# The first expert routing of a fused attention and two-layer expert kernel, cut into more steps and spread over one more attention round, with two elementwise parts on GpSimd

## The chip, the cores and the metric

One core of a Trainium2 chip runs the whole program. The metric is the device time of one execution in microseconds (us). The core has a matrix engine (TensorE, PE in the rows; PEld is its weight load), VectorE (DVE), ScalarE (ACT), GpSimd (POOL) and SyncE (SP), each with its own in-order instruction queue, and 16 DMA engines that they feed. The kernel's gathers by index are issued from GpSimd's queue.

## What is computed

```python
def _attn_ref(q, k, v, w_phi):                 # 4 batches, 8 heads, 576 tokens, 64 wide
    def phi(x):
        proj = np.einsum('bhsd,df->bhsf', x, w_phi)                  # 128 features
        proj = proj - np.max(np.abs(proj), axis=-1, keepdims=True)
        return np.concatenate([np.exp(proj), np.exp(-proj)], axis=-1)
    q_p, k_p = phi(q), phi(k)
    kv = np.einsum('bhsf,bhsd->bhfd', k_p, v); z = np.sum(k_p, axis=2)
    num = np.einsum('bhsf,bhfd->bhsd', q_p, kv)
    return num / (np.einsum('bhsf,bhf->bhs', q_p, z)[..., None] + 1e-06)

def _moe_ref(x, modality_id, w_gate, modality_bias, w1, w2):   # 2304 tokens, 512 wide, 8 experts
    logits = x @ w_gate + modality_bias[modality_id]
    e_idx = np.argmax(logits, axis=1)                          # one expert per token
    gate_w = softmax(logits)[e_idx]
    for e in range(8):
        h = np.maximum(x[e_idx == e] @ w1[e], 0.0)             # 1024 hidden
        out[e_idx == e] = gate_w * (h @ w2[e])

def _moe2_ref(x, w_a, w_b, w_out):                             # 1536 hidden
    return ((x @ w_a) * (x @ w_b)) @ w_out
```

## The kernel before

The program has three phases. **Attention** runs in rounds `r` = 0 to 8 (`Attn.round`). Each handles one unit `u` (a batch pair and a pair of heads): round `r` does the first half of unit `r` (`phi`, `turn`, `kx`, and `num` parts (0,0) and (0,1)) and the second half of unit `r - 1` (`num` parts (1,0), (1,1), (2,0), then `store`). Units 0 to 3 are the tokens of half 0, units 4 to 7 those of half 1. In this phase TensorE's instructions go out in the order in which the code writes them; the other engines' orders are set by a scheduler from the dependences and priorities.

In `phi`, TensorE writes `pjp`, VectorE takes its largest magnitude (`m`, L156) and subtracts it (`df`, L157), and ScalarE takes exponentials; `turn` transposes `df` on TensorE (`qtp`, L187) and ScalarE makes `qts`; `kx` multiplies (`kxp`, L211) and VectorE copies the result out (`kx`, L214); `vg` computes the gate's share (`vgp`, copied to `v`, L199); `num` multiplies (`nmp`, L231) and VectorE divides (`rec`, `x`, L237 to L242); `store` sends `x` to DRAM as `xs` and adds the gate's logits on GpSimd (`lgp`, L259 and L261). `kxp`, `vgp`, `nmp` and the routing's `rkp` share two PSUM buffers.

The **routing** of half 0 (class `Route`) is worked in between these rounds. Its steps are `start`, `gate` (bias by modality), `score` (largest logit, one-hot `oh`), `rank` (a running count by matmul, `rkp`), `place` (tile starts), `where` (each token's row `pl` and column `col`), `bounds` (the numbers `meta` that tell each tile's expert and rows, and the sorted place `cq`, `cl`), `table` (a matmul of one-hots, `tbp`, that yields `idx`, the token that stands in each row) and `back` (the same for the way back, `tbq`, that yields `perm` and the gate weights). `onehot` builds the one-hots of `table` and `back` for half 0 on GpSimd, nine instructions each: `tbpl`, `tbph` for the table, `tbql`, `tbqh` for the way back; `tbpr` and `tbqr` are their products with the token numbers. A side table says after which part of which round a step is written: `aside(0)` follows `kx` of the old unit, `aside(1)` follows its `num` and `store`, `aside(2)` ends the round. `late` keeps a step's instructions behind the last `kx` copy (`at.copied`), with a lower priority.

In the **first expert layer** (`Moe`), a tile of 608 rows is fetched by five gathers `xg` (L577, GpSimd's queue, rows of `xs` by `idx`), transposed on TensorE (`mxt`, L589), split on ScalarE and VectorE (`mxh`, `mxl`) and multiplied (`hp`, `yp`) with weights `s` that SyncE loads by `meta`. Half 1 is routed during this phase, on VectorE. In the **second layer** (`Moe2`) TensorE runs `abp` and `op`. The transposes of the first tile are put into the attention's last part: the first stands behind `kxp` of round 7, ahead of that round's last `nmp`.

Of the kernel before, what the change touches and what calls it, by code (L numbers as in the profile page):

```python
# [58 lines left out]
class Attn:  # L59
# [159 lines left out]
    def num(self, u, *parts):  # L219
# [20 lines left out]
        for b, h in parts:  # L240
            k = 4 if b < 2 else 2
            nc.vector.tensor_mul(x[:, 4 * b:4 * b + 4, h, :] if b < 2 else x[:, 8, :, :], ps[:, o:o + k, 0:72],  # L242
                                 rec[:, o:o + k].unsqueeze(2).to_broadcast([P, k, 72]))
            o += k
# [91 lines left out]
class Route:  # L336
    def __init__(self, tc, pool, lgp, bs, bp):
        self.tc, self.nc = tc, tc.nc
        self.pool, self.lgp, self.bs, self.bp = pool, lgp, bs, bp
# [798 lines left out]
```

## Time and profile before

| | |
|---|---|
| median of 3 runs (lowest to highest) | 821.34 us (820.34 to 823.38) |
| the profiled execution's own time | 816.26 us |
| its span in the profile | 814.5 us |
| busy share of PE, DVE, ACT, POOL | 98%, 74%, 46%, 16% |
| attention until the first `hp` | 163.4 us |
| mean granted TensorE clock | 0.997 of full speed |

The span runs from the first to the last instruction that the profile shows; the execution's own time is 1.8 us longer. Times in the rows are microseconds from the span's start.

### The profile page before, as it was taken

What the parts mean: (1) busy time and instruction counts of PE and PEld (TensorE: products, weight loads), DVE (VectorE), ACT (ScalarE), POOL (GpSimd) and SP (SyncE); (2) the same over time, 40 slices, a digit from 0 to 9 for tenths busy, and PEclk for the clock granted to TensorE, in tenths of its full rate; (3) what the DMA queues carried; (4) which work ended last, traced back from release to release, by engine and by line L of the source; (5) the groups of instructions that cost most, each with busy time, mean ns of one, the idle gap of its engine ahead of it and who ended that gap; (6) DMA issues with size and microseconds to landing.
All of it is one profiled execution on the core that took longest, in us unless ns stands there. A gap on an engine that the chain in (4) does not pass through costs nothing.

```text
span 814.5 us, 18323 instructions
## 1 busy us (share of the span) xinstructions
PE 796.5 (98%) x7284; PEld 750.3 (92%) x7284; DVE 602.4 (74%) x1071; ACT 376.0 (46%) x666; POOL 134.1 (16%) x164
## 2 busy tenths in 40 slices
PE   8999998999999999999999999999999999999996
PEld 6999898899999999999999899999999999999995
DVE  6888899799999999972798787864455686544553
ACT  4556544545345646443554434643333364333333
POOL 2000009532245532200220100030000002000002
PEclk9999999999999999999999999999999999999998
DMA  8665442586589887761889787785566658665642
GB/s 296 211 187 172 153 123 72 150 276 230 200 280 354 325 283 277 265 240 66 329 302 353 257 301 268 259 285 197 189 222 211 201 182 299 210 202 191 211 133 88
DMA packets 85164, 184.22 MB, mean 226 GB/s; under 512 B 27761, under 2 KB 37521, under 8 KB 85073
## 3 DMA queue, kind: packets, MB, share of 16 engines
q1 hardware_dynamic: 81872, 173.21, 62.1%
q0 software_dynamic: 3040, 9.72, 3.4%
q8 instruction: 58, 0.95, 0.5%
q14 instruction: 34, 0.27, 0.1%
q10 hardware_dynamic: 160, 0.07, 0.0%
HBM read 145.21 MB, written 37.75 MB: 225 GB/s over the span
## 4 chain that ended last, share of the span: by engine, by line
PE 32%; issue 16%; DVE 1%; ACT 1%; DMA 1%; POOL 1%; POOLq 0%; DVEq 0%
PE abp L54 7%; PE abp L56 7%; PE abp L55 7%; PE op L55 4%; PE op L54 4%; PE op L56 4%; DMA raw<-in_moe_w 1%; POOL out L853 1%; ACT pc L897 0%; DVE gl L885 0%; ACT gh L884 0%; DVE ca L883 0%; ACT yh L797 0%; DVE o L850 0%; POOLq L1135 0%
## 5 line engine op out<-in xcount | busy, mean ns | idle before, releaser
L897 ACT COPY pc<-abp 128x384 f32<-128x384 f32 x252 | 120.6, 479 | 189.9 <-PE abp L56 187.3
L54 PE MATMUL abp<-yh,fw 128*128 128x384 f32 x504 | 170.0, 337 | 2.7 <-ACT pc L897 1.7
L56 PE MATMUL abp<-yh,fw 128*128 128x384 f32 x504 | 170.0, 337 | 0.0
L55 PE MATMUL abp<-yl,fw 128*128 128x384 f32 x504 | 169.8, 337 | 0.0
L54 PEld LDWEIGHTS abp<-yh,fw 128*128 128x128 f32 x504 | 94.6, 188 | 12.0 <-ACT pc L897 2.7
L55 PEld LDWEIGHTS abp<-yl,fw 128*128 128x128 f32 x504 | 94.7, 188 | 7.5
L56 PEld LDWEIGHTS abp<-yh,fw 128*128 128x128 f32 x504 | 94.6, 188 | 0.0
L717 POOL TENSOR_SCALAR cvs<-cvs 128x768 f32<-128x768 f32 x24 | 58.1, 2419 | 198.9 <-ACT cvs L716 198.9
L55 PE MATMUL op<-fw,gh 128*128 128x512 f32 x216 | 85.6, 397 | 0.0
L54 PE MATMUL op<-fw,gh 128*128 128x512 f32 x216 | 85.1, 394 | 0.0
L56 PE MATMUL op<-fw,gl 128*128 128x512 f32 x216 | 85.0, 393 | 0.0
L55 PE MATMUL yp<-hl,wh 128*128 128x304 f32 x256 | 77.4, 303 | 0.6 <-DVE hl L608 0.6
L54 PE MATMUL hp<-mxh,wh 128*128 128x304 f32 x256 | 77.9, 305 | 0.0
L55 PE MATMUL hp<-mxl,wh 128*128 128x304 f32 x256 | 77.8, 304 | 0.0
L56 PE MATMUL hp<-mxh,wl 128*128 128x304 f32 x256 | 77.7, 304 | 0.0
L56 PE MATMUL yp<-hh,wl 128*128 128x304 f32 x256 | 77.6, 304 | 0.0
L54 PE MATMUL yp<-hh,wh 128*128 128x304 f32 x256 | 77.0, 303 | 0.0
L853 POOL DMA_INDIRECT out<-o,perm x18 | 18.4, 1020 | 332.8 <-ACT o L852 326.0
L190 ACT ACTIVATE qts<-qtp 128x512 f32<-128x512 f32 (+1 forms) x80 | 38.3, 558 | 57.8 <-PE qtp L187 49.6
L908 DVE TENSOR_TENSOR d<-u,pc 128x768 f32<-128x768 f32 x36 | 34.5, 957 | 29.1 <-ACT pc L897 29.1
L885 DVE TENSOR_TENSOR gl<-ca,gh 128x384 fp32r<-128x384 f32 x72 | 39.9, 559 | 19.9 <-ACT gh L884 19.0
L884 ACT CAST gh<-ca 128x384 fp32r<-128x384 f32 x72 | 36.7, 514 | 36.5 <-DVE ca L883 36.4
(191 smaller groups left out, 1599.0 us busy)
## 6 DMA issues: line engine op xcount, KB each, us to landing
fw<-wsc SPq DMA_DIRECT2D x72, 512.0 KB, 4.3
fw<-wsc SPq DMA_DIRECT2D x144, 256.0 KB, 3.4
raw<-in_moe_w SPq DMA_DIRECT2D x24, 768.0 KB, 6.1
s<-in_moe_w SPq DMA_DIRECT2D x32, 512.0 KB, 5.0
fw<-wsc SPq DMA_DIRECT2D x72, 128.0 KB, 2.9
wsc<-whi SPq DMA_DIRECT2D x12, 640.0 KB, 6.3
wsc<-wsum SPq DMA_DIRECT2D x12, 640.0 KB, 7.0
wsc<-whi SPq DMA_DIRECT2D x12, 512.0 KB, 3.2
```

Of the source, the lines that this page charges most:

```text
L54: nc.tensor.matmul(out, lh, rh, start=start, stop=False)
L55: nc.tensor.matmul(out, lh, rl, start=False, stop=False)
L56: return nc.tensor.matmul(out, ll, rh, start=False, stop=stop).ins
L190: nc.scalar.activation(t[:, s, :n, :], ps[:, :n, :], AF.Exp, scale=1.0 - 2.0 * s)
L717: nc.gpsimd.tensor_scalar(out=s.bitcast(F32), in0=s.bitcast(F32), scalar1=LEAST, scalar2=None, op0=ALU.max)
L853: st = nc.gpsimd.indirect_dma_start(out=self.out[:, :], out_offset=bass.IndirectOffsetOnAxis(ap=self.routes[bp].perm[:, c:c + 1], axis=0), ...
L884: nc.scalar.copy(gh, ca[:, i, :])
L885: self.gl = nc.vector.tensor_sub(gl, ca[:, i, :], f32(gh)).ins
L897: copied = nc.scalar.copy(x, ps).ins
L908: nc.vector.tensor_add(d, u, x.unsqueeze(1).to_broadcast([P, 2, n]))
```

## The change

`Route.steps` has twelve steps instead of nine. `place` makes one of the two prefix sums; the other goes with the spans' comparisons and differences to the new step `spans`. The sorted place goes to `sort`, and `bounds` keeps the reductions that make `meta`. The gate's normaliser and its split into three bf16 parts go from `rank` and `back` to `norm`. For half 0, `eng` is GpSimd: seven of `gate`'s eight instructions and five of `spans` run there (`b2` is two instructions instead of one, and the product has a tile `span` of its own). Half 1 keeps VectorE. `where` and `bounds` are held behind the last scaled `x` (`at.scaled`) instead of the last `kx` copy.

| step | before: after round, aside | now |
|---|---|---|
| start, gate | 4, 2 | 4, 2 |
| score | 5, 0 | 5, 0 |
| rank, place | 5, 2 | 5, 2 |
| where | 6, 0 | 6, 1 |
| bounds (before), spans (now) | 6, 2 | 6, 2 |
| sort | part of bounds | 7, 0 |
| bounds, table | 6, 2 and 7, 0 | 7, 1 |
| norm | part of rank and back | 7, 2 |
| back | 8, 0 | 8, 0 |

```diff
+        self.eng = tc.nc.vector if bp else tc.nc.gpsimd
...
-        return [start, self.gate, self.score, self.rank, self.place, self.where, self.bounds, self.table, self.back]
+        return [start, self.gate, self.score, self.rank, self.place, self.where, self.spans, self.sort, self.bounds, self.table, self.norm, self.back]
...
-        nc.vector.tensor_copy(mf, mi)
+        eng.tensor_copy(mf, mi)
...
         for m in range(2):
-            nc.vector.tensor_scalar(out=sel, in0=mf, scalar1=float(m), scalar2=None, op0=ALU.is_equal)
-            nc.vector.tensor_mul(tmp, sel.unsqueeze(2).to_broadcast([P, NG, E]),
+            eng.tensor_scalar(out=sel, in0=mf, scalar1=float(m), scalar2=None, op0=ALU.is_equal)
+            eng.tensor_mul(tmp, sel.unsqueeze(2).to_broadcast([P, NG, E]),
                                  bb[:, m, :].unsqueeze(1).to_broadcast([P, NG, E]))
-            nc.vector.tensor_add(lg, lg if m else self.lgp, tmp)
+            eng.tensor_add(lg, lg if m else self.lgp, tmp)
...
-        pf = self.w([2, E], "pf")
-        for i in range(2):
-            nc.vector.tensor_mul(big, c["m8"], tv[:, i, :].unsqueeze(1).to_broadcast([P, E, E]))
-            nc.vector.tensor_reduce(out=pf[:, i, :], in_=big, op=ALU.add, axis=AX.X)
-        self.tv, self.pf, self.vals = tv, pf, self.w([3, NG], "vals")
+        self.tv, self.pf, self.vals = tv, self.w([2, E], "pf"), self.w([3, NG], "vals")
+        self.prefix(0)
...
+    def prefix(self, i):
+        nc, big = self.nc, self.w([E, E], "big")
+        nc.vector.tensor_mul(big, self.cst["m8"], self.tv[:, i, :].unsqueeze(1).to_broadcast([P, E, E]))
+        nc.vector.tensor_reduce(out=self.pf[:, i, :], in_=big, op=ALU.add, axis=AX.X)
+
+    def sort(self):
+        nc, c, pf = self.nc, self.cst, self.pf
         of = self.pick(2, pf[:, 1, :].unsqueeze(1).to_broadcast([P, NG, E]))
         pc = self.w([NG], "pc")
         nc.vector.tensor_add(pc, of, self.vals[:, 0, :])
         self.cq = self.floordiv(pc, c["kp"][:, 1:NG], "cq")
         self.cl = self.over(pc, self.cq, P, "cl")
...
+    def spans(self):
+        nc, c, tv, pf, eng = self.nc, self.cst, self.tv, self.pf, self.eng
+        self.prefix(1)
...
         nc.vector.tensor_add(end, te_, tv[:, 0, :])
...
+        eng.tensor_sub(lo, lo, hi)
+        eng.tensor_scalar(out=b2, in0=te_, scalar1=-float(TS), scalar2=None, op0=ALU.mult)
+        eng.tensor_add(b2, b2, of_)
+        eng.tensor_add(span, c["ittS"].unsqueeze(2).to_broadcast([P, NTMAX, E]),
+                       b2.unsqueeze(1).to_broadcast([P, NTMAX, E]))
+        eng.tensor_mul(span, span, lo)
...
-def late(tc, step, at):
+def late(tc, step, at, scaled=False):
     def run():
-        with tc.high_priority(offset=-LOWR), tc.issue_after(at.copied):
+        with tc.high_priority(offset=-LOWR), tc.issue_after(at.scaled if scaled else at.copied):
             step()
...
-                rsteps = [low(tc, rsteps[0])] + [late(tc, st, at) for st in rsteps[1:7]] + [low(tc, rsteps[7])]
+                rsteps = [(late(tc, st, at, i in (5, 8)) if i not in (0, 9) else low(tc, st)) for i, st in enumerate(rsteps[:11])]
...
-            at.round(r, {4: {2: rsteps[:2]}, 5: {0: rsteps[2:3], 2: rsteps[3:5]}, 6: {0: rsteps[5:6], 2: rsteps[6:7]},
-                         7: {0: rsteps[7:8]}, 8: {0: rsteps[8:]}}.get(r, {}) if r > 2 else {})
+            at.round(r, {4: {2: rsteps[:2]}, 5: {0: rsteps[2:3], 2: rsteps[3:5]}, 6: {1: rsteps[5:6], 2: rsteps[6:7]},
+                         7: {0: rsteps[7:8], 1: rsteps[8:10], 2: rsteps[10:11]}, 8: {0: rsteps[11:]}}.get(r, {}) if r > 2 else {})
```

On GpSimd, from the one-hots of the table to the first gathers of the first expert layer's first tile, before:

```order
L484 TENSOR_SCALAR tbpl<-i_1744,pl 128x128 x2
L484 TENSOR_SCALAR tbph<-icol,col 128x45 x9
L484 TENSOR_SCALAR tbpl<-i_1744,pl 128x128 x7
L496 TENSOR_TENSOR tbpr<-tbph,tokp 128x9x45 x2
L259 TENSOR_TENSOR lgp_96<-lgp_96,x 128x72
L261 TENSOR_TENSOR lgp_96<-lgp_96,x 128x72
L484 TENSOR_SCALAR tbqh<-icol,cqq 128x9 x9
L484 TENSOR_SCALAR tbql<-i_1744,cl 128x128 x9
L496 TENSOR_TENSOR tbqr<-tbqh,tokp 128x9x9 x2
L496 TENSOR_TENSOR tbqr<-tbqh,gp 128x9x9 x3
L577 DMA xg<-xs_63,idx_2627 128x512 x2
```

And the same stretch of GpSimd's queue now:

```order
L491 TENSOR_SCALAR tbpl<-i_1744,pl 128x128 x2
L491 TENSOR_SCALAR tbph<-icol,col 128x45 x9
L491 TENSOR_SCALAR tbpl<-i_1744,pl 128x128 x7
L469 TENSOR_TENSOR b_2508<-b_2508,pf 128x8
L467 TENSOR_TENSOR lo<-lo,hi 128x72
L503 TENSOR_TENSOR tbpr<-tbph,tokp 128x9x45 x2
L470 TENSOR_TENSOR span<-ittS,b_2508 128x72
L472 TENSOR_TENSOR span<-span,lo 128x72
L491 TENSOR_SCALAR tbqh<-icol,cqq 128x9 x9
L491 TENSOR_SCALAR tbql<-i_1744,cl 128x128 x9
L503 TENSOR_TENSOR tbqr<-tbqh,tokp 128x9x9 x2
L259 TENSOR_TENSOR lgp_96<-lgp_96,x 128x72
```

Behind the last of these rows stand the first two gathers. Four instructions of `spans` have come in between, the logits of unit 5 now stand ahead of the stretch and those of unit 6 within it, and the products with `gp` have gone behind the gathers; both families of one-hots still stand ahead of the first gather.

On VectorE, round 6, from the last scaled `x` of unit 5 to the copy `v`, now (before, the eight rows from `jtc` to the second `col` stood right behind the preceding `kx`, eleven rows ahead of this `x`):

```order
L242 TENSOR_TENSOR x<-nmp,rec 128x144
L433 TENSOR_TENSOR jtc<-vals,kts 128x9
L436 TENSOR_REDUCE jtq<-jtc 128x9
L441 SCALAR_TENSOR_TENSOR rc<-jtq,vals 128x9
L421 TENSOR_TENSOR col<-vals,jtq 128x9
L433 TENSOR_TENSOR jbc<-rc,kp 128x36
L156 TENSOR_REDUCE m<-pjp 128x8
L436 TENSOR_REDUCE jbq<-jbc 128x9
L157 TENSOR_TENSOR df<-pjp,m 128x1024
L441 SCALAR_TENSOR_TENSOR pl<-jbq,rc 128x9
L422 SCALAR_TENSOR_TENSOR col<-col,jbq 128x9
L214 COPY kx<-kxp 128x292
```

`pl` and `col`, which GpSimd's one-hots read, are now written after the round's last `df`. Behind the last row stand `spans`' five VectorE rows and then the copy `v`.

On TensorE, the end of round 7 now, from its last `kxp` on (before, eight `mxt`, two sub-tiles, stood where four stand here first):

```order
L211 MATMUL kxp<-v,kt 64x73 x2
L603 MATMUL mxt<-ident,xg 128x128 x4
L231 MATMUL nmp<-kx,qts 64x73 x32
L187 MATMUL qtp<-ident,df 128x128 x8
L603 MATMUL mxt<-ident,xg 128x128 x6
L211 MATMUL kxp<-v,kp 64x73 x8
```

The first sub-tile's transposes keep their place ahead of `nmp`; the second's and half of the third's now stand behind `qtp`.

## Rows read from the trace of the kernel before

**Rows 1.** The page: busy time, share of the span and instructions by engine.
```profile
PE 796.5 (98%) x7284; PEld 750.3 (92%) x7284; DVE 602.4 (74%) x1071; ACT 376.0 (46%) x666; POOL 134.1 (16%) x164
```

**Rows 2.** Windows, TensorE: stretch, length, busy, instructions, granted clock, DMA share, GB/s.
```profile
72.62:90.87 18.25, 18.25 (x436) 1.00 0.55 170
111.23:131.25 20.02, 18.71 (x446) 1.00 0.31 91
```

**Rows 3.** Timeline of TensorE: start, duration, operation, [idle before, releaser].
```profile
91.89 2.30 PE L231 MATMUL nmp<-kx,qts 128*64 128x73 f32 x64
...
107.62 1.09 PE L187 MATMUL qtp<-ident,df 128*128 128x128 f32 x8 [0.48 <-DVE df L157]
...
114.75 0.21 PE L391 MATMUL rkp<-oh,ltri 128*128 128x80 bf16 x1 [0.27 <-DVE x L242]
...
127.64 1.09 PE L187 MATMUL qtp<-ident,df 128*128 128x128 f32 x8 [1.04 <-DVE df L157]
...
134.80 1.24 PE L231 MATMUL nmp<-kx,qts 128*64 128x73 f32 x32 [1.31 <-DVE meta L466]
...
148.26 1.09 PE L187 MATMUL qtp<-ident,df 128*128 128x128 f32 x8 [0.36 <-DVE df L157]
...
151.97 1.09 PE L589 MATMUL mxt<-ident,xg 128*128 128x128 f32 x8
```

**Rows 4.** Timeline of VectorE, the ends of rounds 4 and 6 and what leads to the latter.
```profile
91.09 0.46 DVE L214 COPY kx<-kxp 128x292 f32<-128x292 f32 x1
...
121.43 0.16 DVE L438 TENSOR_TENSOR jtc<-vals,kts 128x9 f32<-128x9 f32 x1
...
122.65 1.22 DVE L156 TENSOR_REDUCE m<-pjp 128x8 f32<-128x1024 f32 x1
...
128.50 0.67 DVE L242 TENSOR_TENSOR x<-nmp,rec 128x288 f32<-128x288 f32 x2
...
131.85 1.29 DVE L431 TENSOR_TENSOR sel<-oh,pf 128x72 f32<-128x72 bf16 x1
...
134.36 0.29 DVE L199 COPY v<-vgp 128x144 f32<-128x144 f32 x1
```

**Rows 5.** Timeline of GpSimd, from the table's one-hots to the first gather.
```profile
122.77 1.21 POOL L484 TENSOR_SCALAR tbpl<-i,pl 128x128 bf16<-128x128 f32 x2 [13.20 <-DVE col L427]
...
131.32 1.68 POOL L496 TENSOR_TENSOR tbpr<-tbph,tokp 128x405 bf16<-128x405 bf16 x2
132.96 0.37 POOL L259 TENSOR_TENSOR lgp<-lgp,x 128x72 f32<-128x72 f32 x1
...
135.10 2.68 POOL L484 TENSOR_SCALAR tbqh<-icol,cqq 128x9 bf16<-128x9 f32 x9 [1.32 <-DVE cqq L441]
...
143.50 0.87 POOL L496 TENSOR_TENSOR tbqr<-tbqh,gp 128x81 bf16<-128x81 bf16 x3
144.53 1.11 POOL L577 DMA_INDIRECT xg<-xs,idx  x1 [0.16 <-issue]
```

**Rows 6.** DMA issues: the gathers at 144.53 and at 152.04, us to landing.
```profile
xg<-xs,idx POOLq DMA_INDIRECT x1, 3.8
...
xg<-xs,idx POOLq DMA_INDIRECT x1, 5.4
```

**Rows 7.** Timeline of TensorE, its last matmul and its first; windows at the end.
```profile
807.35 0.39 PE L56 MATMUL op<-fw,gl 128*128 128x512 f32 x1
...
810.25:810.50 0.25, 0.00 (x0) 0.00 (x0) 0.00 (x0) 0.00 (x0) 0.00 (x0) 0.50 0.01 0
...
1.27 3.75 PE L973 MATMUL warmp<-warm 128*128 128x512 bf16 x9 [1.27 <-DVE warm L970]
10.42 0.82 PE L178 MATMUL idp<-warm 128*128 128x512 bf16 x3
```

**Rows 8.** One line and one tile: least, median and longest ns.
```profile
L431 DVE TENSOR_TENSOR sel<-oh,pf x4: 216/220/1287, 118.1 to 207.7; 128x72 f32<-128x72 bf16 x4
L717 POOL TENSOR_SCALAR cvs<-cvs x24: 2127/2162/4663, 169.9 to 456.9; 128x768 f32<-128x768 f32 x24
```

More of the change, by code (lines that the diff above doesn't have):

```diff
@@ L241, in num @@
             k = 4 if b < 2 else 2
[L242 to L243 removed]
+            self.scaled = nc.vector.tensor_mul(x[:, 4 * b:4 * b + 4, h, :] if b < 2 else x[:, 8, :, :], ps[:, o:o + k, 0:72],
+                                 rec[:, o:o + k].unsqueeze(2).to_broadcast([P, k, 72])).ins
             o += k
@@ L455, in bounds @@
         self.cl = self.over(pc, self.cq, P, "cl")
-        lo = self.w([NTMAX, E], "lo")
-        hi = self.w([NTMAX, E], "hi")
+    def spans(self):
+        nc, c, tv, pf, eng = self.nc, self.cst, self.tv, self.pf, self.eng
+        self.prefix(1)
         te_, of_ = pf[:, 0, :], pf[:, 1, :]
-        end = self.w([E], "end")
+        lo, hi, span = (self.w([NTMAX, E], n) for n in ("lo", "hi", "span"))
+        end, b2 = self.w([E], "end"), self.w([E], "b2")
+        it = c["it"].unsqueeze(2).to_broadcast([P, NTMAX, E])
@@ new lines, in spans, with bounds @@
+        eng.tensor_scalar(out=b2, in0=te_, scalar1=-float(TS), scalar2=None, op0=ALU.mult)
[3 more added lines that the diff above has]
+        eng.tensor_mul(span, span, lo)
+        self.hi, self.span, self.end = hi, span, end
+    def bounds(self):
+        nc = self.nc
+        meta = self.w([3 * NTMAX + 1], "meta")
+        nc.vector.tensor_reduce(out=meta[:, :NTMAX], in_=self.hi, op=ALU.add, axis=AX.X)
+        nc.vector.tensor_scalar(out=meta[:, :NTMAX], in0=meta[:, :NTMAX], scalar1=float(E - 1), scalar2=None, op0=ALU.min)
+        nc.vector.tensor_reduce(out=meta[:, NTMAX:2 * NTMAX], in_=self.span, op=ALU.add, axis=AX.X)
@@ L474, in bounds @@
         nc.vector.tensor_scalar(out=meta[:, 2 * NTMAX:3 * NTMAX], in0=meta[:, NTMAX:2 * NTMAX], scalar1=float(CG),
                                 scalar2=float(HALF), op0=ALU.add, op1=ALU.min)
-        nc.vector.tensor_copy(meta[:, 3 * NTMAX:], end[:, E - 1:E])
+        nc.vector.tensor_copy(meta[:, 3 * NTMAX:], self.end[:, E - 1:E])
         self.meta = self.pool.tile([1, 3 * NTMAX + 1], I32, name=f"meta{self.bp}")
@@ L515, in table, with norm @@
         self.token(self.idx, hi, lo, 0)
-    def back(self, ps=None, tag=None):
+    def norm(self):
         nc = self.nc
-        gp = self.w([3, NG], "gp", BF16)
+        gt = self.gt = self.w([NG], "gt")
+        nc.vector.tensor_reduce(out=gt, in_=self.ex, op=ALU.add, axis=AX.X)
+        nc.vector.tensor_scalar_add(gt, gt, 1e-9)
+        nc.vector.reciprocal(gt, gt)
+        gp = self.gp = self.w([3, NG], "gp", BF16)
         rest = self.w([NG], "grest")
@@ L525, in back @@
                 nc.vector.tensor_sub(rest, rest, gp[:, i, :])
+    def back(self, ps=None, tag=None):
+        nc, gp = self.nc, self.gp
         self.g2 = self.pool.tile([P, NG], F32, name=f"g2{self.bp}")
@@ L1019, in trn_kernel @@
         side = {}
-        for f, k in enumerate((0, 0, 0, 2, 4, 4, 4, 8, 8)):
+        for f, k in enumerate((0, 0, 0, 2, 4, 4, 4, 4, 4, 8, 8, 8)):
             side.setdefault(k, []).append(low(tc, rs[f]))
```

21 lines of the change are left out of this document (3 added, 18 removed).

## The prediction

> **What bounds the kernel now.** The page's busy shares come first: TensorE is busy 98% of the span, the next engine, VectorE, 74% [rows 1]. So time is won or lost only where TensorE waits or is given other work, and what delays it in attention is not given back later: the expert layers behind attention are TensorE's as well. The windows by round come second. A round without routing, 72.62 to 90.87, takes 18.25 us and TensorE is busy through all of it; round 6's, 111.23 to 131.25, takes 20.02 us with 18.71 busy [rows 2]. Third, TensorE's timeline names the holes in the routing rounds: 0.48 (behind `score`), 0.27, 1.04, 1.31 and 0.36 us, each ended by a VectorE instruction [rows 3]. The last four, which the change can touch, sum to 2.98 us, 0.36% of the time: that is nearly all there is to win. Fourth, GpSimd's timeline: from 122.77 to 144.53 it makes one-hots, and the first gather of the first expert tile stands behind them [rows 5]. It lands 3.8 us after its issue [rows 6], at 148.3, and TensorE transposes it at 151.97 without a wait [rows 3]. So the gather is 3.6 us early. That slack belongs to the change's price.
>
> **The change part by part.**
>
> *Gate on GpSimd.* It takes seven VectorE instructions away at the end of round 4, behind the `kx` of 91.09 [rows 4]. TensorE's next hole on VectorE's account comes only at 107.62, a round later [rows 3], so I take nothing. On GpSimd the seven cost about 0.4 us each by the nearest row, the 0.37 us logit sums [rows 5], and nothing is queued behind them until round 5 ends. A gain is excluded, since no hole lies behind them; a loss of up to 7 x 0.4 = 2.8 us would need `score` to wait for them, but `score` comes some 8 us later.
>
> *Norm out of round 5's end.* `rkp` waited 0.27 us for a scaled `x` [rows 3], which nine small norm instructions had delayed. I take 0.15 us won; 0 to 0.27.
>
> *Where out of round 6's start.* Eight instructions stood ahead of `m`, 121.43 to 122.65, so 1.22 us [rows 4]; TensorE then waited 1.04 us for `df` [rows 3]. Gone with them: 1.04 won.
>
> *Where in its new place.* The same eight instructions now stand ahead of and among the round's last `m`, `df` and `kx`, and `num` waits for `kx`. Eight times 0.16, less what overlaps, is about 1.15 us; at the end of round 4 `kx` was done at 91.55 [rows 4] and `num` started at 91.89 [rows 3], so 0.34 us of it is hidden, less some signalling. I take 0.95 us lost; 0 to 1.3.
>
> *Bounds out of round 6's end.* `v` was copied at 134.36 behind eleven such instructions, the first of which, `sel`, took 1.29 us [rows 4], and `num` waited 1.31 us for it, for a PSUM buffer [rows 3]. Five instructions of `spans` are left ahead of `v`, about 0.8 us, and `v` should come just in time: 1.31 won.
>
> *Sort and bounds in round 7.* `sort` puts five instructions ahead of an `m`, as `score` did in round 5, where TensorE waited 0.48 us [rows 3]. The 0.36 us there now go [rows 3]. I take 0.1 lost.
>
> So TensorE comes to the first transpose about 0.15 + 1.04 - 0.95 + 1.31 - 0.1 = 1.45, with what rounds off say 1.6 us earlier: at 150.4 instead of 151.97.
>
> *The gather.* Now the same chain on GpSimd. `pl` and `col` were done at 122.7, just ahead of `tbpl` [rows 5]. Now they come behind the last `x`, the `m` and the `df` of round 6. The last `x`, at 128.50 [rows 4], ended at 129.17; it moves up with round 6 by 1.3 us to about 127.9. Five `where` instructions (0.75), `m` (1.2), `df` (1.2) and the last two (0.2) give 131.3. So `tbpl` starts at 131.4 instead of 122.77. From there: one-hots of the table as before, 131.32 - 122.77 = 8.55 [rows 5], to 139.95; the sum into `b2` and the difference `lo`, two logit-sized operations, 0.7, to 140.65; `tbpr`, 132.96 - 131.32 = 1.64, to 142.3; the span's sum and product, 0.8, to 143.1; the one-hots and token products of the way back, 143.50 - 135.10 = 8.40, to 151.5; one logit sum, 0.4, to 151.9; issue, 0.16, to 152.1 [rows 5]. The first gather goes out 7.6 us later than now. It lands 3.8 us later in the quiet case and 5.4 us in the case beside stores of `xs`, as at 152.04 [rows 6]; `meta`, for which the loads of `s` wait, is now made in round 7 too, so these loads run beside it, and I take 4.6. That is 156.7, and the transpose starts at 156.8: **4.8 us later** than at 151.97, with 4.0 and 5.6 for the two landings. TensorE has stood since 150.4, that is 6.4 us. What follows the transpose is the same work in about the same order, and the later gathers go out 1.11 + 0.16 us apart [rows 5], ahead of their transposes, so nothing more is lost there and nothing is given back.
>
> *The clock.* So long a hole does not occur in the trace between the first and last matmul. Behind the last one, which ends at 807.7, the granted clock is at 0.50, the lower level (1.2 GHz), by 810.25, after 2.5 us of rest [rows 7]. A hole of 6.4 us should do the same. What it costs to come back, the start shows: nine 512-column matmuls took 3.75 us, 0.42 us apiece, whereas three of the same kind at 10.42 took 0.82 us with the drain of the last, about 0.22 apiece [rows 7]. So 9 x 0.2 = **1.8 us** were lost. I take that; the bounds are 0 (the clock stays) and twice it (3.6).
>
> *Contention.* VectorE and GpSimd share something: `sel` took 1.287 us instead of 0.22 [rows 8] while `tbpr` ran from 131.32 to 132.96 [rows 4, 5], and it ended only when both of `tbpr`'s instructions had. GpSimd's `cvs` went from 2.1 to 4.7 us [rows 8]. The four two-operand instructions of `spans` on VectorE now fall into 8.5 us of one-hots. At one one-hot of 0.6 us each (1.21 us for two [rows 5]) that would be 2.4 us, all of it inside TensorE's later wait for the gather, so it doesn't enter the sum. The Trainium skill, "SBUF — State Buffer", section "SBUF: two separate sides", says that the port pair that VectorE and GpSimd share is locked for one whole instruction, also by a VectorE operation with two SBUF inputs against a GpSimd operation that reads SBUF, and that the other is blocked until then. By that rule the price is these 2.4 us; the row on `sel`, which sat out two GpSimd instructions, is harsher, and a rival below takes it at its word.
>
> *Sum.* 4.8 + 1.8 = 6.6 us. The profiled execution, 816.26 us, would read 822.9. The median of the runs shown, 821.34, lies 5.1 us above it, and the changed kernel will be timed as those were, so I forecast 821.34 + 6.6 = **827.9 us**, 0.8% slower. What can be told from no change in this kernel is about 0.5%, 4.1 us.
>
> **The rivals.**
>
> *The gather waits, the clock stays.* For it: a hole of 6.4 us can shrink to about 4 by contention, and the trace has no hole of such a length ahead of its end to go by. Against it: the 2.5 us at the end. 821.34 + 4.8 = 826.1 us.
>
> *The one-hots hold VectorE.* If VectorE's first two-operand instruction of `spans`, near 131.6, gets no turn until the one-hots end at 139.95, `v` and the second `num` part come 8.3 us late; `sort` then gives `cqq` at about 149, GpSimd reaches it at 143.1 and waits 5.9, the gather goes out at 158.0 and the transpose starts at 162.7. That is 10.7 and with the clock 12.5 us: 833.8 us. For it: `sel` [rows 4]. Against it: GpSimd's `cvs` was itself the one delayed in many cases [rows 8], so the lock changes hands.
>
> *Not slower.* The gather hides after all and only the shorter rounds count: 1.6 us won, 819.7 us. It needs the first gather's issue at 150.4 - 3.8 = 146.6 or earlier, 5.5 us ahead of my sum. The way there would be `pl` done by 126, that is in round 6 ahead of `x`. Against it: the rows of the new order, and nine one-hots of 0.6 us ahead of the gather.
>
> **How the numbers follow.** Forecast 63%, clock stays 17%, one-hots hold VectorE 8%, not slower 12%. The range: from below, a landing of 3.8 us and no clock loss is +4.0, less 1.5 us by which my walk through round 6 may place `pl` too late: 823.8. From above, a landing of 5.4 us (+0.8), GpSimd slowed by VectorE by 1 us (estimate, from `cvs` [rows 8]) and twice the clock loss (+1.8): 6.6 + 3.6 = 10.2, so 831.5. It leaves out the last two cases, 20%. Slower by over 0.5%: 60 of the forecast's 63, 10 of the 17, all 8: 0.78. Faster: 0.04 of the last case's 0.12, if rounds gain more than I see. The rest, 0.18, is no change.
>
> **What would show it.** Right: GpSimd's first `tbpl` at about 131.4 and first gather at about 152; TensorE's first `mxt` near 157 with an idle stretch of 4 to 7 us ahead of it; the granted clock at 0.5 for some us from there; rounds 5 to 7 with holes of under 1 us; the first `hp` near 170 instead of 163.4. Wrong, if the first gather goes out before 147, if TensorE's order lets other work into the hole, or if the second half gives time back (the stretch from first `hp` to the end is now 814.5 - 163.4 = 651.1 us and should stay within 1 us).

## The result, and the profile after

The changed kernel takes 826.3 us (median of 9 runs, 823.75 to 828.93); the kernel before took 821.34 us beside it (9 runs, 819.20 to 824.27). The ratio is 1.0059, interval 1.0045 to 1.0073: 0.6% slower, 5.0 us by the medians. In after_again below, on another chip, the ratio was 1.0083 (1.0057 to 1.0109). The forecast of 6.6 us lies between the two. The profiled execution took 826.09 us, its span 824.3 us; before's span was 814.5 us. So the two profiles are 9.8 us apart, twice as much as the medians, and an experiment below asks why.

The page's busy line, against [rows 1]: TensorE has 5.9 us more of busy time for the same work, GpSimd and VectorE next to no change.
```profile
PE 802.4 (97%) x7283; PEld 754.6 (92%) x7284; DVE 602.6 (73%) x1061; ACT 376.3 (46%) x666; POOL 133.9 (16%) x176
```

The timeline of TensorE in the changed kernel, against [rows 3] (start, duration, operation, [idle before, releaser]):
```profile
106.72 1.09 PE L187 MATMUL qtp<-ident,df 128*128 128x128 f32 x8 [0.47 <-DVE df L157]
...
113.63 0.21 PE L392 MATMUL rkp<-oh,ltri 128*128 128x80 bf16 x1
...
125.45 1.09 PE L187 MATMUL qtp<-ident,df 128*128 128x128 f32 x8
...
130.75 2.25 PE L231 MATMUL nmp<-kx,qts 128*64 128x73 f32 x64 [0.51 <-DVE big L446]
...
147.16 0.84 PE L507 MATMUL tbp<-tbpr,tbpl 128*128 128x90 bf16 x9 [3.87 <-DVE rec L237]
147.92 2.08 PE L154 MATMUL pjp<-wp,qk 64*128 64x128 f32 x16
149.94 1.97 PE L187 MATMUL qtp<-ident,df 128*128 128x128 f32 x8
...
157.85 0.27 PE L211 MATMUL kxp<-v,kt 128*64 128x73 f32 x1 [0.49 <-issue]
158.05 0.66 PE L603 MATMUL mxt<-ident,xg 128*128 128x128 f32 x4
158.76 3.86 PE L231 MATMUL nmp<-kx,qts 128*64 128x73 f32 x64
...
172.57 0.39 PE L54 MATMUL hp<-mxh,wh 128*128 128x304 f32 x1
```
The attention rounds did what was forecast: no wait at `rkp`, none at round 6's `qtp` (125.45), and one of 0.51 us ahead of `num`'s first part, where 1.31 stood ahead of its second. Then TensorE stands 3.87 us in front of `tbp`, which the forecast did not have, and works at half speed behind it (`qtp` 1.97 us instead of 1.09). The first `mxt` comes at 158.05 instead of 151.97, and behind it `nmp` takes 3.86 us, where 2.25 is normal. The first `hp` is at 172.57 instead of 163.4.

GpSimd's timeline, against [rows 5]:
```profile
130.25 1.22 POOL L491 TENSOR_SCALAR tbpl<-i,pl 128x128 bf16<-128x128 f32 x2 [1.95 <-DVE col L422]
...
139.26 1.71 POOL L503 TENSOR_TENSOR tbpr<-tbph,tokp 128x405 bf16<-128x405 bf16 x2
...
141.69 2.71 POOL L491 TENSOR_SCALAR tbqh<-icol,cqq 128x9 bf16<-128x9 f32 x9
...
150.13 0.34 POOL L259 TENSOR_TENSOR lgp<-lgp,x 128x72 f32<-128x72 f32 x1
150.63 1.12 POOL L591 DMA_INDIRECT xg<-xs,idx  x1 [0.16 <-issue]
```
That is the forecast's chain: `tbpl` at 130.25 (forecast 131.4), the first gather at 150.63 (152.1). This execution reached round 5 0.90 us earlier than the one that the forecast was read from (106.72 and 107.62 in the `qtp` rows), so `tbpl` is 0.25 us ahead of the forecast and the gather 0.6.

The windows (length, TensorE's busy time, granted clock, DMA share, GB/s) show the clock at its lower level of 1.2 GHz twice, the first time in and behind the wait at `tbp`, the second behind five short holes ahead of `mxt` (0.32 to 0.49 us; the last is the row at 157.85). The page calls such a hole issue: the engine waited for nothing that the profile shows.
```profile
146.00:152.00 6.00, 4.84 (x35) 0.50 0.24 55
...
160.00:162.00 2.00, 2.00 (x38) 0.50 0.39 131
```

From the first `hp` to the end it is 824.3 - 172.6 = 651.7 us, against 651.1 before. So nearly all that was lost was lost ahead of the first `hp`, and half 1's routing behind it, which the change cuts into twelve steps too, costs next to nothing more.

### The profile page after: what moved, and what is told of

The parts are those of the page before. It is cut to its first block, busy times and chain, and to the rows that moved or that the text cites. A ratio compares the mean times of both kernels' runs of the same rounds, so it can differ in the third digit from the quotient of the medians.

```text
span 824.3 us, 18320 instructions
## 1 busy us (share of the span) xinstructions
PE 802.4 (97%) x7283; PEld 754.6 (92%) x7284; DVE 602.6 (73%) x1061; ACT 376.3 (46%) x666; POOL 133.9 (16%) x176
## 3 DMA queue, kind: packets, MB, share of 16 engines
q1 hardware_dynamic: 81872, 173.21, 61.6%
## 4 chain that ended last, share of the span: by engine, by line
issue 41%; PE 6%; POOL 2%; DVE 1%; POOLq 0%; ACT 0%
POOL out L867 2%; PE abp L54 2%; PE abp L56 1%; PE abp L55 1%; PE op L55 1%; PE op L54 1%; PE op L56 1%; POOL cvs L731 0%; POOLq L1149 0%; DVE gl L899 0%; DVE cvs L746 0%; DVE cvt L744 0%; DVE wsum L749 0%; DVE cvs L747 0%; ACT gh L898 0%
## 5 line engine op out<-in xcount | busy, mean ns | idle before, releaser
L898 ACT CAST gh<-ca 128x384 fp32r<-128x384 f32 x72 | 36.7, 514 | 36.5 <-DVE ca L897 36.4
```

What stands on the lines that cost most here:

```text
L898: nc.scalar.copy(gh, ca[:, i, :])
```

## The experiments

They ran on three chips, numbered 14 (before_again, table_q, bounds_late, where_back), 5 (after_again, bounds_back, where_alone, early_meta, gate_norm) and 11 (gather_first, back_behind, gate_alone); the record names none for the result above. Each was timed beside the kernel before, whose median there was 816.8 to 817.2 us. Executions reach round 5 at times that differ by up to 4.5 us, so the last three columns count from the start of round 5's `qtp` (the first row of each timeline, 106.72 above) in the same trace. The ratio is that of the timed runs, with its interval. Diffs are against the changed kernel, those of where_alone, gate_alone and gate_norm against the kernel before, and show the lines that matter (... for what is left out). In the changed kernel `rsteps[5]` to `rsteps[11]` are `where`, `spans`, `sort`, `bounds`, `table`, `norm` and `back`; in the kernel before `rsteps[5]` to `rsteps[8]` are `where`, `bounds`, `table` and `back`.

| kernel | ratio to before | first gather out | first `mxt` | first `hp` |
|---|---|---|---|---|
| before (the profile shown) | | 36.9 | 44.4 | 55.8 |
| before_again | | 36.9 | 44.3 | 55.8 |
| changed (the profile above) | 1.0059 (the result) | 43.9 | 51.3 | 65.9 |
| after_again | 1.0083 (1.0057 to 1.0109) | 43.9 | 50.0 | 64.3 |
| table_q | 1.0077 (1.0056 to 1.0098) | 43.9 | 49.6 | 63.7 |
| bounds_late | 1.0093 (1.0074 to 1.0112) | 43.9 | 47.5 | 61.6 |
| bounds_back | 1.0057 (1.0038 to 1.0075) | 44.0 | 47.7 | 60.0 |
| where_alone | 1.0070 (1.0052 to 1.0089) | 43.9 | 47.5 | 61.9 |
| where_back | 1.0044 (1.0027 to 1.0061) | 34.1 | 43.2 | 59.9 |
| gather_first | 1.0036 (1.0020 to 1.0052) | 42.5 | 46.2 | 60.2 |
| early_meta | 1.0013 (1.0001 to 1.0024) | 34.7 | 43.8 | 57.2 |
| back_behind | 1.0081 (1.0055 to 1.0107) | 34.6 | 43.8 | 60.0 |
| gate_alone | 0.9989 (0.9973 to 1.0006) | 36.9 | 44.0 | 55.4 |
| gate_norm | 0.9978 (0.9966 to 0.9990) | 36.7 | 43.9 | 55.4 |

**Three theories.** 1: the first gather's late issue on GpSimd sets the first `mxt` (the forecast). 2: TensorE's own path does, that is the wait at `tbp` and the lower clock behind it. 3: the gather goes out late and besides lands late, since the loads of the first weights, `s`, now go out with it.

**before_again: the profile of before once more.**

> The kernel before, profiled once more. The profiled execution on record, 816.3 us, lies 5.1 us under the median of 821.3. If the stages up to the first hp vary from one execution to the next, an execution near 821 us shows its first hp later than 163.4 us, and part of the 9.8 us between the two profiles is chance; if the experts vary, the first hp stays at 163.4 within 1 us and the stretch behind it is longer than 651 us. I expect the second.

It took 815.62 us, with the first `hp` at 162.7 and 651.1 us behind it: the same execution again, and neither case of the expectation. The median of before's timed runs beside it, 817.01 us, is only 1.4 us above. So why before's timed runs beside the result lie 5.1 us above its profile no trace shows, and it stays open. But the profiled execution (816.26 us) is none of those nine runs (819.20 to 824.27), while it fits the runs of before on the three chips here (814.47 to 820.46); the changed kernel's profiled execution is one of its nine. That the profiles' difference of 9.8 us overstates the change, where the result was timed, follows from the medians alone.

**after_again: the changed kernel beside the others.**

> The changed kernel once more, as the measure for the runs beside it: 1.006 of the kernel before, so 822 us where before takes 817 us; the first hp 8 to 9.5 us later than before's. The holes called issue stand again in kxp beside the loads of s, if they belong to the program and not to chance.

The ratio is 1.0083. TensorE's timeline, VectorE's, and the first gather's issue with its us to landing:
```profile
148.94 0.54 PE L507 MATMUL tbp<-tbpr,tbpl 128*128 128x90 bf16 x9 [3.88 <-DVE rec L237]
...
158.46 0.66 PE L603 MATMUL mxt<-ident,xg 128*128 128x128 f32 x4 [2.58 <-DMA xg<-xs,idx]
159.05 3.49 PE L231 MATMUL nmp<-kx,qts 128*64 128x73 f32 x64
162.47 1.45 PE L187 MATMUL qtp<-ident,df 128*128 128x128 f32 x8
...
169.24 2.76 PE L231 MATMUL nmp<-kx,qts 128*64 128x73 f32 x80 [1.39 <-DVE kx L214]
```
```profile
168.03 0.69 DVE L607 TENSOR_TENSOR mxl<-mxt,mxh 128x512 fp32r<-128x512 f32 x1 [4.58 <-ACT mxh L606]
...
168.78 0.40 DVE L214 COPY kx<-kxp 128x292 f32<-128x292 f32 x1
```
```profile
xg<-xs,idx POOLq DMA_INDIRECT x1, 6.0
```
Here the gather is what `mxt` waits for. In the first profile, holes called issue in `kxp` from 154.89 to 157.85 had hidden that; they are absent here, so they belong to that execution and not to the program. The gather takes 6.0 us to land; it took 3.8 before [rows 6]. TensorE's two waits, 3.88 and 2.58, make 6.46 us: the forecast's one hole of 6.4, in two pieces. The last wait, 1.39 us, was 0.23 in before: VectorE's `mxl` stands ahead of `kx` on its queue and waits 4.58 us for a subtile whose transposes the order splits into 6 and 2.

**table_q: the wait at `tbp` taken away.**
```diff
-        hi, lo = self.lookup("tbp", self.col, n, self.pl, self.toks)
+        hi, lo = self.lookup("tbp", self.col, n, self.pl, self.toks, *((None, None) if self.bp else self.tps))
...
+                routes[0].tps = (at.ps_q, "q")
```

> The changed kernel with the sums of the table (tbp) in another PSUM buffer, the one of qtp, so that TensorE need not wait for VectorE's x; the order of TensorE and GpSimd is the same. Theory 1 (the first gather on GpSimd's queue sets the first transpose): tbp starts near 143.3 instead of 147.2, the first gather still goes out at about 150.6, the first transpose comes at 157 to 158, and the time stays within 1 us of 826.3. Theory 2 (TensorE's own path sets it: the wait for the PSUM buffer and the half clock behind it): the first transpose comes 3.5 to 4 us earlier and the time is about 822.5 us.

Its TensorE timeline:
```profile
45.90 0.28 PE L211 MATMUL kxp<-v,kt 128*64 128x73 f32 x1 [1.94 <-issue]
...
103.03 0.41 PE L211 MATMUL kxp<-v,kp 128*64 128x73 f32 x5 [1.54 <-issue]
...
147.31 0.55 PE L507 MATMUL tbp<-tbpr,tbpl 128*128 128x90 bf16 x9
...
150.69 0.63 PE L187 MATMUL qtp<-ident,df 128*128 128x128 f32 x4 [1.23 <-DVE rec L238]
152.70 0.82 PE L187 MATMUL qtp<-ident,df 128*128 128x128 f32 x4 [1.39 <-DVE idx L515]
...
160.37 1.11 PE L603 MATMUL mxt<-ident,xg 128*128 128x128 f32 x4 [2.76 <-DMA xg<-xs,idx]
```
The wait at `tbp` is gone, others come for VectorE (1.23, 1.39), and `mxt` waits for the gather again: 49.6 instead of 50.0 behind round 5. The time is that of after_again (ratios 1.0077 and 1.0083). Theory 2 falls: TensorE's wait at `tbp` costs nothing, since without it TensorE waits for the gather instead.

**bounds_late: the loads of `s` held back behind the gathers.**
```diff
-                         7: {0: rsteps[7:8], 1: rsteps[8:10], 2: rsteps[10:11]}, 8: {0: rsteps[11:]}}.get(r, {}) if r > 2 else {})
+                         7: {0: rsteps[7:8], 1: rsteps[9:10], 2: rsteps[10:11]}, 8: {0: [rsteps[8], rsteps[11]]}}.get(r, {}) if r > 2 else {})
```

> The changed kernel with bounds one round later, so that the first expert's weights are loaded some 12 us behind the first gathers instead of together with them. Theory 3 (the loads of s and the gathers together hold up the gather's landing and TensorE's instruction fetch): the holes called issue in kxp between 154 and 158 are gone, the first gather lands in about 4 us instead of 6.6, and the first transpose comes 1.5 to 2.5 us earlier than 158.05. Theories 1 and 2: the gather lands as late as before and the holes stay. Of the time I expect little, since the weights come later and the first hp may wait for them: 824 to 829 us.

GpSimd's timeline and TensorE's:
```profile
150.34 1.12 POOL L591 DMA_INDIRECT xg<-xs,idx  x1 [0.17 <-issue]
```
```profile
153.89 0.66 PE L603 MATMUL mxt<-ident,xg 128*128 128x128 f32 x4
...
168.04 0.41 PE L54 MATMUL hp<-mxh,wh 128*128 128x304 f32 x1 [1.41 <-ACT wh L582]
```
The gather went out at 150.34 and `mxt` runs at 153.89 without a wait, so it landed in at most 3.55 us: 2.5 us of `mxt`'s delay (47.5 instead of 50.0) came from the loads. The gain is lost at the other end, as expected: the weights are late, the first `hp` waits 1.41 us for `wh`, the next ones for `wl` and `x`.

**bounds_back: the loads of `s` ahead of the gathers, as before.** For that `bounds` and `spans` return to the end of round 6 and `spans` to VectorE.
```diff
-        nc, c, tv, pf, eng = self.nc, self.cst, self.tv, self.pf, self.eng
+        nc, c, tv, pf, eng = self.nc, self.cst, self.tv, self.pf, self.nc.vector
...
-                rsteps = [(late(tc, st, at, i in (5, 8)) if i not in (0, 9) else low(tc, st)) for i, st in enumerate(rsteps[:11])]
+                rsteps = [(late(tc, st, at, i == 5) if i not in (0, 9) else low(tc, st)) for i, st in enumerate(rsteps[:11])]
...
-            at.round(r, {4: {2: rsteps[:2]}, 5: {0: rsteps[2:3], 2: rsteps[3:5]}, 6: {1: rsteps[5:6], 2: rsteps[6:7]},
-                         7: {0: rsteps[7:8], 1: rsteps[8:10], 2: rsteps[10:11]}, 8: {0: rsteps[11:]}}.get(r, {}) if r > 2 else {})
+            at.round(r, {4: {2: rsteps[:2]}, 5: {0: rsteps[2:3], 2: rsteps[3:5]}, 6: {1: rsteps[5:6], 2: [rsteps[6], rsteps[8]]},
+                         7: {0: rsteps[7:8], 1: rsteps[9:10], 2: rsteps[10:11]}, 8: {0: rsteps[11:]}}.get(r, {}) if r > 2 else {})
```

> The changed kernel with spans and bounds in their old place and on VectorE, at the end of round 6; sort, where, table, norm and gate stay as changed. The loads of s go out near 138 to 141, before the gathers. Theory 3 (loads of s and gathers together hold up the landing and the instruction fetch): no issue holes in kxp behind 150, the first gather lands in about 4 us, the first transpose comes 3 to 4 us earlier than in the changed kernel and, other than with bounds_late, the first hp too; round 6 gives back about 1 us in front of num, so 2 to 3 us under the changed kernel, 1.003 of before. Theories 1 and 2: the landing stays at 5.5 us or more, and the time within 1 us of the changed kernel's or above it.

The gather's us to landing, TensorE's timeline, and GpSimd's:
```profile
xg<-xs,idx POOLq DMA_INDIRECT x1, 3.6
```
```profile
155.09 0.66 PE L603 MATMUL mxt<-ident,xg 128*128 128x128 f32 x4 [0.20 <-DMA xg<-xs,idx]
...
156.95 2.25 PE L231 MATMUL nmp<-kx,qts 128*64 128x73 f32 x64
```
```profile
142.52 2.70 POOL L491 TENSOR_SCALAR tbqh<-icol,cqq 128x9 bf16<-128x9 f32 x9 [1.19 <-DVE cqq L436]
```
The gather leaves as late as in the changed kernel (44.0 behind round 5) and `mxt` comes 2.3 us earlier, since it lands in 3.6 us. TensorE then waits only 0.20 us, the clock does not fall a second time (`nmp` 2.25 us), and the first `hp` comes 4.3 us earlier. The time falls too, by 3.8 us by the medians (824.54 to 820.74) and by 2.1 by the ratios, whose intervals overlap (1.0057 to 1.0109 and 1.0038 to 1.0075). Theory 3 stands by the traces: the new place of `bounds` and `spans` is worth 4.3 of the 8.5 us that the first `hp` is late, although their old place costs a wait in round 6; what it is worth in timed runs is less sure. The last row shows why the gather leaves no sooner, though `spans` no longer stands on GpSimd's queue: GpSimd waits 1.19 us for `sort`'s `cqq` instead.

**where_alone: `where` and `table` moved, nothing else.**
```diff
...
-                rsteps = [low(tc, rsteps[0])] + [late(tc, st, at) for st in rsteps[1:7]] + [low(tc, rsteps[7])]
+                rsteps = [low(tc, rsteps[0])] + [late(tc, st, at, i == 4) for i, st in enumerate(rsteps[1:7])] + [low(tc, rsteps[7])]
...
-            at.round(r, {4: {2: rsteps[:2]}, 5: {0: rsteps[2:3], 2: rsteps[3:5]}, 6: {0: rsteps[5:6], 2: rsteps[6:7]},
-                         7: {0: rsteps[7:8]}, 8: {0: rsteps[8:]}}.get(r, {}) if r > 2 else {})
+            at.round(r, {4: {2: rsteps[:2]}, 5: {0: rsteps[2:3], 2: rsteps[3:5]}, 6: {1: rsteps[5:6], 2: rsteps[6:7]},
+                         7: {1: rsteps[7:8]}, 8: {0: rsteps[8:]}}.get(r, {}) if r > 2 else {})
```

> The kernel before with where and table alone moved as in the change; gate, norm, bounds and sort stay. Theory 1, as forecast for this part: GpSimd's tbpl at 130 to 131, the first gather at 148.5 to 150.5 (no difference operations of spans on GpSimd), the first transpose 3 to 5 us later than before's 152, and 1.004 to 1.006 of before. If Theory 3 carries half of the loss, the landing is 4 us here, since meta and the loads of s are early, and the part alone costs 2 to 3 us, 1.003 of before.

The gather's us to landing, and TensorE's timeline:
```profile
xg<-xs,idx POOLq DMA_INDIRECT x1, 3.6
```
```profile
146.76 0.54 PE L500 MATMUL tbp<-tbpr,tbpl 128*128 128x90 bf16 x9 [1.76 <-DVE rec L237]
...
155.13 0.66 PE L589 MATMUL mxt<-ident,xg 128*128 128x128 f32 x4 [1.43 <-DMA xg<-xs,idx]
156.89 0.66 PE L589 MATMUL mxt<-ident,xg 128*128 128x128 f32 x4 [1.10 <-DMA xg<-xs,idx]
157.48 3.88 PE L231 MATMUL nmp<-kx,qts 128*64 128x73 f32 x64
```
With an early `meta` the gather lands in 3.6 us, and this part alone still costs 5.9 us by the medians (822.72 against 816.83), more than Theory 3's "2 to 3". The gather is 7.0 us late and has 3.6 of slack; `mxt` is 3.1 late. The rest is behind it: the second transposes wait too (1.10), and the clock falls (`nmp` 3.88).

**where_back: the change without these two.**
```diff
-                rsteps = [(late(tc, st, at, i in (5, 8)) if i not in (0, 9) else low(tc, st)) for i, st in enumerate(rsteps[:11])]
+                rsteps = [(late(tc, st, at, i == 8) if i not in (0, 9) else low(tc, st)) for i, st in enumerate(rsteps[:11])]
...
-            at.round(r, {4: {2: rsteps[:2]}, 5: {0: rsteps[2:3], 2: rsteps[3:5]}, 6: {1: rsteps[5:6], 2: rsteps[6:7]},
-                         7: {0: rsteps[7:8], 1: rsteps[8:10], 2: rsteps[10:11]}, 8: {0: rsteps[11:]}}.get(r, {}) if r > 2 else {})
+            at.round(r, {4: {2: rsteps[:2]}, 5: {0: rsteps[2:3], 2: rsteps[3:5]}, 6: {0: rsteps[5:6], 2: rsteps[6:7]},
+                         7: {0: [rsteps[9], rsteps[7]], 1: rsteps[8:9], 2: rsteps[10:11]}, 8: {0: rsteps[11:]}}.get(r, {}) if r > 2 else {})
```

> The changed kernel with where and table in their old places (gate, norm, spans, sort and bounds stay as changed). Theory 1: GpSimd's tbpl starts near 122 us, the first gather goes out at 144 to 146, the first transpose comes at about 150.5 without a wait, and what is left of the change is a gain: 820 us, 1 to 2 us under before. Theory 3: the late meta still puts the loads of s among the gathers, holes called issue stay in kxp, and the time is 822 to 824 us.

GpSimd's timeline and TensorE's:
```profile
152.14 1.04 POOL L591 DMA_INDIRECT xg<-xs,idx  x1 [0.15 <-issue]
```
```profile
149.57 1.09 PE L603 MATMUL mxt<-ident,xg 128*128 128x128 f32 x8
...
157.53 1.08 PE L603 MATMUL mxt<-ident,xg 128*128 128x128 f32 x4 [2.58 <-DMA xg<-xs,idx]
```
The first transposes come 1.1 us earlier than in before, as Theory 1 had it, and yet the kernel is slower, 1.0044, which no theory had. The first two gathers leave at 140.41 and 141.83, the third only at 152.14, behind the one-hots of the way back, and beside the loads of `s`; TensorE waits 2.58 us for it. In before all five leave behind these one-hots, the last ones ahead of their transposes.

**gather_first: bounds_back with the gather earlier on GpSimd's queue.** It has table_q's PSUM buffer as well, and its extra lines make `tbqh` wait for the table:
```diff
+            cq = self.w([NG], "cqd")
+            self.nc.vector.scalar_tensor_tensor(out=cq, in0=t[:, :NG], scalar=0.0, in1=self.cq, op0=ALU.mult, op1=ALU.add)
+            self.cq = cq
```

> As bounds_back (spans and bounds in their old place on VectorE; where, table, norm and sort as changed), and in addition the table's sums in qtp's PSUM buffer and the one-hots of the way back behind the first two gathers on GpSimd. Theory 1 (the first gather's place on GpSimd's queue): the first gather goes out about 2 to 2.5 us earlier than in bounds_back, the first transpose comes as much earlier, and the time is 1.002 to 1.003 of before, where bounds_back had 1.0057. If the first transpose does not move with the gather, TensorE's own path has become the bound and the time stays at 1.005.

GpSimd's timeline and TensorE's:
```profile
142.59 5.22 POOL L491 TENSOR_SCALAR tbql<-i,cl 128x128 bf16<-128x128 f32 x9 [2.39 <-DVE cl L441]
...
148.76 1.11 POOL L596 DMA_INDIRECT xg<-xs,idx  x1 [0.63 <-DMA xs<-x]
```
```profile
152.53 0.66 PE L608 MATMUL mxt<-ident,xg 128*128 128x128 f32 x4 [1.25 <-DMA xg<-xs,idx]
```
The gather leaves 1.5 us earlier and `mxt` comes 1.5 us earlier, 3.77 us behind it: Theory 1, one to one. It is less than the 2 to 2.5 us expected, since only `tbqh` went behind the gather: `tbql` stayed ahead of it, after 2.39 us of waiting for `sort`'s `cl`. The first `hp` did not follow in the profile (60.2 against 60.0), because the second transposes wait 0.90 us and the clock falls; the ratio, 1.0036, has an interval that overlaps bounds_back's.

**early_meta and back_behind: the parts that looked free.** The first leaves `where`, `table`, `spans` and `bounds` in place and moves gate, `norm` and `sort`; the second also puts the one-hots of the way back behind the gathers. In both, `spans` runs on VectorE. The places in early_meta, then what back_behind adds:
```diff
...
+            at.round(r, {4: {2: rsteps[:2]}, 5: {0: rsteps[2:3], 2: rsteps[3:5]}, 6: {0: rsteps[5:6], 2: [rsteps[6], rsteps[8]]},
+                         7: {0: [rsteps[9], rsteps[7]], 2: rsteps[10:11]}, 8: {0: rsteps[11:]}}.get(r, {}) if r > 2 else {})
```
```diff
+                    with tc.issue_after(at.added):
+                        routes[0].back(at.ps_q, "q")
...
+                         7: {0: [rsteps[9], rsteps[7]], 2: rsteps[10:11]}, 8: {1: rsteps[11:]}}.get(r, {}) if r > 2 else {})
```

> The kernel before with gate's elementwise part on GpSimd, norm out of round 5 and sort out of round 6's end; where, table, spans and bounds stand where they stood. All theories: tbpl near 122, the first gather ahead of the one-hots of the way back at 141 to 142, the loads of s ahead of the gathers, the first transpose 1 to 1.5 us earlier than before's, no wait there: 0.998 of before. If it is at 1.000 or above, the holes that VectorE makes in TensorE are filled by others.

> As early_meta (where, table, spans and bounds in their old places, gate on GpSimd, norm and sort later), with the one-hots of the way back and their sums put behind the first five gathers. In early_meta the third gather stood behind the one-hots, went out at 154.1 and TensorE waited 1.8 us for it. Expected: third gather at 147 to 149, no wait of TensorE for a gather, first hp at about 162.3 instead of 165.0, and 0.998 to 0.999 of before. If a wait for tbq takes its place, 1.001 as before.

TensorE's timeline in early_meta, and in back_behind TensorE's and GpSimd's:
```profile
157.66 0.63 PE L603 MATMUL mxt<-ident,xg 128*128 128x128 f32 x4 [1.77 <-DMA xg<-xs,idx]
```
```profile
167.12 0.39 PE L507 MATMUL tbq<-tbqr,tbql 128*128 128x45 bf16 x9 [4.26 <-POOL tbqr L503]
```
```profile
156.08 7.11 POOL L491 TENSOR_SCALAR tbql<-i,cl 128x128 bf16<-128x128 f32 x9
```
Both miss their ratios (0.998 and 0.998 to 0.999 expected; the case with the wait for `tbq` was put at 1.001 and came to 1.0081). Moving `sort` lets the first two gathers pass the one-hots, which then hold up the third (1.77 us). With the one-hots behind the gathers, `tbq` waits for them instead, 4.26 us: they start later, and `tbql` takes 7.11 us instead of 5.24. On GpSimd's queue whichever stands last is waited for; before's order is the best of those tried.

**gate_alone and gate_norm: work on GpSimd where it is idle.**
```diff
+        self.eng = tc.nc.vector if bp else tc.nc.gpsimd
...
-            nc.vector.tensor_mul(tmp, sel.unsqueeze(2).to_broadcast([P, NG, E]),
+            eng.tensor_mul(tmp, sel.unsqueeze(2).to_broadcast([P, NG, E]),
...
-            nc.vector.tensor_copy(gp[:, i, :], rest)
+            self.eng.tensor_copy(gp[:, i, :], rest)
```

> The kernel before with gate's elementwise part on GpSimd alone. The prediction took nothing for it: 1.000 of before, within 0.0015, the first hp within 0.5 us of before's at equal issue holes. The bound from the other side was a loss of 2.8 us, 1.0034.

> The kernel before with gate's elementwise part and the copies and differences of the gate's three parts (gp, grest) on GpSimd, which is idle from 99 to 122 us, and nothing else moved. Expected from the rows: the wait of rkp for VectorE, 0.26 us, goes; where's and bounds' holes of 1.03 and 1.3 us stay; 0.998 to 0.999 of before. If GpSimd's share of VectorE's time matters at this place, 1.000 or more.

Gate alone is worth nothing that can be told. With the copies and differences of `gp` on GpSimd as well, in its idle stretch (timeline of GpSimd in gate_norm),
```profile
112.74 0.19 POOL L522 COPY grest<-gt 128x9 f32<-128x9 f32 x1 [3.01 <-DVE gt L401]
```
`rkp` no longer waits, and the kernel is the only one whose interval lies wholly below 1: 815.06 against 816.97 us, 0.9978. That it beats gate_alone can't be told, since their intervals overlap. The wait that went explains 0.26 us of the 1.9; its first `mxt` and `hp` stand within 0.1 us of gate_alone's and 0.4 of before's, so the rest isn't explained.

## Why the prediction was right, and where it wasn't

*Gate on GpSimd*, taken at nothing: right (gate_alone).

*Rounds 5 and 6.* `norm` gave 0.27 us (taken: 0.15), `where` out of round 6's start 1.04 (1.04), `bounds` out of its end 1.31 (1.31), and `where` in its new place cost 0.51 (0.95): 2.1 us won instead of 1.55. From round 5's `qtp` to round 7's `pjp` it was 28.35 us and is 26.21. Hardly any of it was worth anything, because the gather does not wait for it.

*Sort in round 7*, taken at 0.1 us: this step failed, though by table_q TensorE's wait behind it cost nothing in the end. `sort`'s `pc` ran from 139.19 for 1.82 us, where its other instance took 0.156, while `tbpr`'s two instructions ran from 139.26 to 140.97; `m` came late, then `x`, and `tbp` needs the PSUM buffer that `x` frees. VectorE's timeline in the changed kernel:
```profile
130.73 0.22 DVE L465 TENSOR_TENSOR lo<-it,pf 128x72 f32<-128x72 f32 x1
...
139.19 1.82 DVE L453 TENSOR_TENSOR pc<-vals 128x9 f32<-128x9 f32 x1
...
141.51 1.21 DVE L156 TENSOR_REDUCE m<-pjp 128x8 f32<-128x1024 f32 x1
```
That is the pattern of `sel` [rows 4, 8], at one instruction and not at four: the contention term stayed inside the wait, as said. The Trainium skill, "SBUF — State Buffer", section "SBUF: two separate sides", has the shared port pair locked for one whole instruction; here, as with `sel`, VectorE sat out both of GpSimd's. Beside the one-hots it sat out nothing: the four two-operand instructions of `spans`, which the forecast put at 2.4 us, took 0.16 to 0.31 us each while `tbpl` ran (the row of `lo` is one), so there the trace does not agree with the Trainium skill.

Nor is `sort` all of the wait at `tbp`. In where_alone `sort` is not in round 7, and TensorE still waits 1.76 us there: about 2.1 of the 3.88 us are `sort`'s, and the rest comes of `table`'s new place behind the round's `num`, whose PSUM buffers it shares. For that place the forecast had no term. And `sort` is close to delaying the gather: its `cqq` is done at 141.59, and GpSimd comes to it at 141.69; with less on GpSimd's queue it waits for `sort` (bounds_back, gather_first).

*TensorE stands 6.4 us in front of the transpose*: right as a sum (3.88 + 2.58 = 6.46 in after_again), wrong as a place. That the sum came out is luck: TensorE's other waits up to there fell by 2.98 - 0.51 = 2.47 us instead of 1.6, the gather came 0.8 us later than forecast, and the lower clock behind `tbp`, which the forecast did not have there, took 1.6 us back (`pjp` 1.95 instead of 1.16, `qtp` 1.90 instead of 1.09).

*The gather*, 4.8 us: the mechanism was right and two of its sizes were off. It left 7.0 us later (7.6), since `tbpl` began 0.25 us earlier than I walked and the chain from there took 20.38 us instead of 20.7, and took 6.0 us to land (4.6). With the slack of 3.6 that makes 7.0 + 2.2 - 3.6 = 5.6 us, which is what `mxt` shows in after_again (50.0 - 44.4). I had named the collision with the loads of `s` and priced it at 0.8 us by the row beside stores of `xs`; two loads of 512 KB cost 2.2 to 2.4.

*The clock*, 1.8 us: it fell twice. The first fall cost nothing, since the gather was later still; the second cost 3.49 - 2.25 at `nmp` and 1.45 - 1.09 at `qtp`, 1.6 us. The size is near, but its source was no row at the lower level: in the stretch at the start that I took it from, the windows show a granted clock of 1.00 (the figure behind the busy times of the five engines),
```profile
2.50:5.00 2.50, 2.50 (x7) 0.76 (x5) 0.00 (x0) 0.84 (x1) 2.01 (x15) 1.00 0.95 249
```
so what made those matmuls slow is not shown.

*"Nothing more is lost there"*: wrong by 1.2 us, `num`'s wait of 1.39 us for `kx` instead of 0.23. The order in which a late gather's transposes and `mxl` were put was part of the change, and I took it for about the same.

*The sum.* In the stage itself after_again loses 5.6 + 1.6 + 1.2 = 8.4 us of the 8.5 that its first `hp` is late; timed it lost 7.7 us by the medians (6.8 by the ratio), and in the result 5.0. So 6.6 us was too little for the stage, by the gather's landing and the wait for `kx`, and too much for the result. The time of 827.9 us came as near as it did by luck: the profiled execution was forecast at 822.9 us and took 826.09, 3.2 more, and the 5.1 us by which before's median lies above its profile, which I added, are 0.2 us in the changed kernel. The two errors go against each other. *The rivals*: 826.1 us ("the clock stays") is nearest to the number, but the clock fell; VectorE was held up by 1.66 us, not 8.3; the gather did not hide.

## What to carry over

A step that a second engine's queue depends on has a due time: before it is moved by half a round, walk that queue to the transfer at its end and compare the slack there (here 3.6 us) with the move (7 us), not with the small holes that it leaves on the busiest engine. A step whose result releases transfers is moved together with them, so ask what they will meet: here about half of what the traces lose up to the first `hp` came from two loads that had left 6 us before the gathers and now left with them. Small work moved to an idle engine was free or better here (gate_alone, gate_norm); on a queue with something urgent in it the order is what counts (gather_first, back_behind).

## What the runs showed of the hardware

A gather's time to landing was 3.6 us in bounds_back and where_alone and 3.8 in before, with the weight loads earlier, and 6.0 us in after_again and 5.6 in table_q, with the first of two loads of 512 KB issued within half a microsecond of it.

TensorE has holes called issue at the same few matmuls of `kxp` in most executions, with sizes that change: 0.15 to 1.54 us near 99 to 103, none to 1.94 near 45 (table_q's rows), none to 0.78 near 61 to 63. They move all that follows: the earliest execution here to reach round 5 (gather_first) has 0.43 us of them, the latest (table_q) 3.48, which is 3.05 of the 4.5 us between the two; the rest is not explained. In before's trace one packet of a DMA queue of the kind instruction fell into 98 to 100 us, beside the hole of 1.29; that these holes wait for such packets is argued, not shown.

The granted clock fell to 0.50 behind waits of 2.58 us (after_again), and of 1.43 and 1.10 us close together (where_alone), and did not fall behind 0.20 and 0.62 (bounds_back), nor behind 1.77 alone (early_meta).
